# A new order of the work behind entry 288, in an attention and MLP-mixer kernel that replays a written order

## The chip, the core and the metric

The program runs on one core of one Trainium2 chip. The core has a matrix engine (PE, with its weight loads shown apart as PEld), a vector engine (DVE), a scalar engine (ACT), a general engine (POOL) and a synchronisation engine (SP). Each works through its own list of instructions in order, and they wait for one another by semaphores. Inputs and output lie in the chip's HBM; transfers between it and the on-chip memory are DMAs, issued here by POOL, SP and ACT. The metric is the device time of one execution in microseconds, as the median over runs.

## What is computed

There are 8 samples of 576 positions. A block-causal attention with 8 heads of width 64 gives x (576 x 512 per sample); then an MLP mixer follows, first over the positions and then over the channels. Cut to what matters, the reference is:

```python
scores = np.matmul(q, k.transpose(0, 1, 3, 2)) / np.sqrt(64)       # q, k, v: (8, 8, 576, 64)
mask = block_i >= block_j                                          # blocks of 64 positions
attn = np.exp(np.where(mask, scores, -1e9) - max); attn /= sum     # over the last axis
x = np.matmul(attn, v)  # heads side by side: (8, 576, 512)
h = np.maximum(x.transpose(0, 2, 1) @ w_tok1, 0.0) @ w_tok2        # 576 -> 256 -> 576
u = x + h.transpose(0, 2, 1)
out = u + np.maximum(u @ w_ch1, 0.0) @ w_ch2                       # 512 -> 1536 -> 512
```

## The kernel before

**Operations and the table.** The function first makes a list of 1526 numbered operations, each with its possible engines, the operations that it depends on, and a small function that emits its instructions. Then `placed` walks a table of words, `ORDER`, and the kernel emits the operations in the table's order. A word such as `1479D` means: emit operation 1479 now, on DVE (T is PE, A is ACT, P is POOL, S is SP). Letters behind it, as in `1488Tgd`, name the PSUM banks that the operation takes: a to d are the tiles `mm0` to `mm3`, e to h the tiles `late0` to `late3`. Since every engine works in order, the table fixes the order of each engine's list, which engine does a move that two engines could do, and which bank is used. Waits follow from the data: an engine stands still at the first instruction whose input or buffer is not ready. Nothing decides at run time.

**The stages.** Per sample: q and k are loaded by POOL (L417) and transposed by DVE in 288-column pieces (L440). `score_set` multiplies them on PE (L562) in three sets per group of four heads; it uses the array in strips of 32 rows. ACT takes the exponential out of PSUM (L777). POOL or DVE copies and clears masked parts (L588, L599). `head_out` multiplies by v on PE (L616), `ends_out` does the last 64 rows (L669) with half of the array's columns; DVE divides by the sum (L636 and L642, L691 and L697). `token_up` (L814, L818) and `token_mix` (L913, L944) are the mixer's first half; SP transposes its result by DMA (L980). `channel_up`, `channel_up_half` (L1114) and `channel_up_fast` (L1238) are the first channel product, the last two with seven products in place of eight (differences made by DVE, sums folded from PSUM, L1153, L1271). `channel_down_fast` (L1372) is the second channel product, also with seven products; DVE makes its operand sums (L1354) and folds each result into the output tile `o_sb` (L1396), and SP or ACT writes it (L1438; L1424 for the shared tile of the samples' last 64 rows). Later samples' attention is interleaved on PE with earlier samples' mixer.

**The end of the program.** Three jobs of `channel_down_fast` stand there. Operations 1466 to 1483 are the shared tile of last rows; its writes are 1480, 1481, 1482 and 1483, each of 256 KB from 64 partitions. Operations 1488 to 1504 and 1509 to 1525 are the last sample in two halves: products 1490, 1492, 1494, 1496, 1498, 1500 and 1511, 1513, 1515, 1517, 1519, 1521 (six matmuls each), each followed by the fold with the next number, and writes 1502 and 1523 (256 KB each), 1503, 1504, 1524 and 1525 (128 KB each). Fold 1479 completes the output tile of writes 1482 and 1483.

Of the kernel before, what the change touches and what calls it, by code (L numbers as in the profile page):

```python
# [27 lines left out]
class Plan:  # L28
# [74 lines left out]
    140D 82P 161P 53Td 141D 146A 60Td 147Td 137D 129D 130D 166A 151Tc 152T 148T 134D 46Ta 44Ta 202Tabef 206A 204A
    205A 164D 185D 175Tg 153D 154D 155Th 149D 176D 177D 156D 157D 267Tc 268D 150D 203A 265Tg 167Th 208Tcbfe 266A
    187P 168T 81P 88P 87P 84P 83P 171Tg 89P 210A 269Td 209A 270A 90P 172T 211A 86P 85P 212A 343P 188D 273Tb 189D
    169D 170D 186D 277Th 173D 241Tdcaf 245A 174D 271Tg 10P 274D 244A 242A 275Tb 281Tf 278D 279Th 272D 285Tg 280A
    276D 195Tbdae 198A 197A 4D 282D 5D 286D 283Th 284D 310Tf 319Tg 287Th 288A 316Td 295Ta 317T 318D 320T 196A 243A
    322Th 323T 321A 199A 228Tdcbg 324A 200D 289Te 207D 290T 232A 230A 261D 296T 297A 6D 345D 311T 312D 231A 191P
    229A 192P 301Tc 193P 262D 346P 302T 235Taghb 239A 291A 236A 292Td 293T 233D 190P 194P 201P 344D 304Tb 294D 305T
    348D 234D 298Te 299T 347D 352P 216Td 219Ta 220D 237A 303A 217D 218D 213Tc 222Tg 306A 214D 223D 300A 238A 215D  # L110
    240D 225Th 226D 224D 367Tdebf 370A 227D 221D 313Tc 314T 369A 255Th 315D 373Tagbe 246Tc 368A 353D 371A 375A 354D
    307Td 376A 349P 247D 377A 256D 91P 248D 252Tf 308T 309A 257D 350D 351D 374A 258Tb 253D 360Tcegh 362A 361A 259D
    522P 364A 254D 334Td 249Te 519P 250D 251D 338Tf 393Thcae 260D 428Tb 395A 263D 264D 363A 520D 523D 396A 429D 397A
    394A 398D 426Tc 427A 92P 339T 372P 406Theag 409A 408A 93P 358P 432Tc 524D 433D 434Tb 435D 407A 340T 341D
    400Tceah 410A 430Tg 431D 436Tf 437D 335T 442Tg 404A 444Th 445D 403A 357P 521D 355P 402A 365P 359P 366P 401A
    446Tf 356P 378Tc 379D 387Te 388D 381Th 384Ta 405P 382D 389D 390Tb 447A 443A 380D 528P 391D 383D 392D 438Tg 385D
    399P 423Tc 424D 439A 536Thefb 537A 538A 539A 440Tg 540A 386D 336T 417Ta 425D 325Tc 549Tbfeh 94D 95D 441A 551A
    96D 450D 552A 531P 525P 97D 337D 329Tg 330T 454Tef 532P 553A 685P 451D 550A 533P 418D 535P 331T 411Tb 529D 332D
    527D 412D 413D 326T 420Tg 688P 421D 414Td 457A 460T 461A 469Thb 419D 422D 472A 455Ta 526D 691P 456A 415D 416D
    530D 470Tg 471A 541D 542P 327T 475T 476A 458Tg 452D 328D 453D 473Ta 543Tdhce 700P 459A 462T 687D 464T 474A 479T  # L120
    477T 546A 463D 547A 534P 544A 545A 690D 478D 569Tdgec 573A 572A 571A 701P 689D 480D 602Th 570A 603D 604Tc 605A
    576Thgea 578A 580A 548P 566Td 482T 577A 465D 466D 574D 467T 468A 694P 567D 568D 686D 612Td 613D 483D 582Thagc
    579A 585A 606Tf 857P 586A 557Te 610Td 581D 481D 584A 484Tbg 485Tc 611D 615S 583A 558D 487A 560Ta 559D 448Th 449A
    607D 608Td 486A 561D 609D 614S 490T 488Tf 491A 562D 554Th 692D 489A 563Te 564D 709Tabdc 711A 555D 556D 494T 342S
    565D 495D 492T 493D 575P 593Te 594D 590Th 591D 587Tb 588D 592D 710A 713A 712A 714P 497T 595D 498D 715Tdfca 333S
    589D 854P 599Th 596Te 597D 496A 697P 699P 695D 598D 716A 600D 719A 601D 870P 718A 696D 499D 500D 503Tgd 717A
    501D 504A 702Tebca 704A 616D 620Tfh 698P 623A 706A 863P 505T 693D 860P 705A 703A 707D 626T 627A 635Tab 507Tc
    638A 502D 641T 642A 506D 509T 508D 748Tgafe 751A 511T 617D 510D 512D 749A 859D 618D 858D 954P 752A 750A 513T
    735Tcaeg 736A 739A 708D 867P 770Tf 619D 514D 771A 855D 636Tc 737A 637D 856D 738A 740P 639Tg 515T 516D 742Tecaf
    862D 640A 645T 646D 745A 726Td 727D 643T 644D 865D 746A 720Ta 868P 768Tf 648T 723Tg 769D 721D 744A 728D 724D  # L130
    725D 624Tc 778Tf 722D 779D 774Td 729Tg 730D 731D 625A 628T 649A 776Ta 743A 747P 621Te 622A 777D 780Tg 781A 775D
    732Ta 783S 871Tdefb 874A 873A 875A 733D 629D 772Tg 647D 734D 741P 753Tc 773D 630T 650Tfa 653A 872A 762Tg 631D
    651Tb 652A 861D 759Te 754D 633T 755D 763D 764D 656T 657D 760D 761D 654Tb 634A 655A 878Tgchd 880A 879A 881A 864D
    765Tf 766D 660T 767D 756Te 757D 661D 658T 782S 819Tgf 758D 882A 822A 517S 804Thc 964P 807A 663T 659D 785D 786D
    789Tde 664A 792A 825T 632D 790Tb 787D 826A 662D 665D 951P 965P 960P 808Ta 809A 791A 866P 795T 796D 805Tg 810T
    806A 812T 813D 811A 793Tb 794A 814T 815D 917Thdga 799T 788D 876P 800D 797T 798D 918A 666D 919A 920A 921A 869P
    957P 820Th 817T 818A 823Tg 824A 802T 803A 967P 884Tabdc 888A 886A 821D 885A 887A 883P 667D 829T 827T 669Teh 670A
    830D 832T 956D 833A 828D 953D 904Tdabc 907A 877P 901Tg 668D 906A 902D 905A 955D 903D 908A 963P 952D 1051P 671T
    672D 911Tdabf 912A 914A 961D 895Tg 896D 897D 898Tc 899D 892Te 893D 915A 913A 900D 894D 937Td 938A 889Tg 981Tcafb
    985A 916D 909P 910P 890D 931Te 958D 932D 933D 984A 982A 673Td 891D 934Tg 983A 816A 959D 1057P 968Tecfb 970A 935D  # L140
    966P 936D 674D 972A 922Ta 923D 1054P 971A 924D 925Tg 926D 962D 1060P 927D 969A 675T 676D 928Ta 1066P 929D
    1008Tgfbc 1010A 677T 1011A 973P 1012A 1009A 930D 678D 975Tabfe 977A 979A 1053D 683S 679T 978A 1014Tebdg 1052D
    976A 680D 1015A 1017A 1055D 1016A 831D 939Tf 940D 1001Teacd 1018A 1002A 1004A 1062D 980P 974P 992Tb 986Tf 1003A
# [12 lines left out]
    1279D 1166T 1167A 1187Tc 1177D 1188A 1189T 1190A 1184Tf 1185D 1138Tdb 1198Tge 1292Th 1293D 1141A 1191T 1192D
# [1430 lines left out]
```

## Time and profile before

| | |
|---|---|
| median of 3 runs | 284.12 us (284.1 to 284.63) |
| the profiled execution: span from first to last instruction | 282.2 us |
| PE busy | 275.3 us (98%), 3580 matmuls |
| DVE busy | 238.8 us (85%), 523 instructions |
| ACT busy | 177.8 us (63%) |
| POOL busy | 78.8 us (28%) |
| read from HBM and written to it | 35.85 MB and 9.44 MB |

The profiled execution's span is 1.9 us shorter than the median time: what lies around the first and the last instruction is not in the profile. A line of a group names the source line, the engine, the operation, the tiles and shapes, the count, the busy time and the mean of one; behind the bar stands the engine's idle time before it. The chain of waits follows the work that ended last backwards, to what released each piece. A matmul's record is longer than the distance to the next one, since they are pipelined; so PE's speed is read from the starts.

### The profile page before, as it was taken

To read this page: it belongs to the slowest core of one execution; us is meant where nothing else is said; L and a number is where in the kernel's file an instruction comes from. 1 tells how busy PE (TensorE), PEld (TensorE's weight loads), DVE (VectorE), ACT (ScalarE), POOL (GpSimd) and SP (SyncE) were. 2 spreads that over 40 slices of the span, in tenths; PEclk is the share of its full clock that TensorE was granted. 3 is DMA by queue.
4 is the path that set the end of the run, shared out by engine and by line. 5 is a ranking of instruction groups with operands and counts; after the bars stand their busy time and mean duration, and the time that the engine had idled before them with its cause. 6 is when DMAs were issued, how large, how long until landed. Compare 5 with 4: busy or idle time off the path is not lost.

```text
span 282.2 us, 8544 instructions
## 1 busy us (share of the span) xinstructions
PE 275.3 (98%) x3580; PEld 193.2 (68%) x3580; DVE 238.8 (85%) x523; ACT 177.8 (63%) x326; POOL 78.8 (28%) x131
## 2 busy tenths in 40 slices
PE   7899999999999999999999999999999999999994
PEld 2457665475768877888776658744589664788884
DVE  4589598889889989999988879887797898898974
ACT  4788888775899774899997990326840858530000
POOL 8876726371613422092257210000000000000000
PEclk9999999999999999999999999999999999999999
DMA  8999999959958947699399465150127200020555
GB/s 160 167 153 194 191 200 203 162 63 170 95 88 229 150 67 56 151 104 127 46 118 161 31 141 120 42 114 19 37 49 210 80 0 0 3 75 14 212 126 174
DMA packets 64918, 31.75 MB, mean 112 GB/s; under 512 B 53104, under 2 KB 56176, under 8 KB 64880
## 3 DMA queue, kind: packets, MB, share of 16 engines
q0 software_dynamic: 45040, 17.64, 54.0%
q1 hardware_dynamic: 19408, 12.91, 16.7%
q10 hardware_dynamic: 432, 0.66, 0.7%
q8 instruction: 28, 0.46, 0.7%
q14 instruction: 10, 0.08, 0.1%
HBM read 35.85 MB, written 9.44 MB: 160 GB/s over the span
## 4 chain that ended last, share of the span: by engine, by line
PE 82%; DMA 10%; DVE 3%; ACT 2%; POOL 1%; issue 1%; DVEq 0%; POOLq 0%
PE mm L1372 13%; PE late L1372 11%; DMA qk_sb<-in_q_dram 7%; PE late L1114 7%; PE late L1238 6%; PE mm L1114 6%; PE mm L1238 6%; PE mm L562 4%; PE late L616 3%; DMA wc_sb<-in_moe_w_ch_dram 3%; PE late L562 3%; PE late L913 3%; PE mm L814 2%; PE mm L616 2%; PE late L814 2%; PE mm L913 2%
## 5 line engine op out<-in xcount | busy, mean ns | idle before, releaser
L777 ACT ACTIVATE e_sb<-mm 128x512 bf16<-128x512 f32 x94 | 53.5, 612 | 9.8 <-PE mm L562 4.2
L777 ACT ACTIVATE e_sb<-late 128x512 bf16<-128x512 f32 x74 | 43.0, 613 | 5.6 <-PE late L562 2.7
L440 DVE STREAM_TRANSPOSE qk_sb<-qk_sb 128x288 int32<-128x288 int32 (+2 forms) x57 | 38.3, 695 | 6.0 <-ACT qk_sb L393 1.9
L469 POOL DMA_DIRECT2D vals<-in_v_dram x45 | 37.1, 833 | 8.5 <-PE late L616 7.5
L1372 PEld LDWEIGHTS <-sums 128*128 128x128 bf16 x288 | 27.8, 98 | 4.2 <-issue 0.4
L1372 PEld LDWEIGHTS <-gT 128*128 128x128 bf16 x288 | 27.9, 98 | 3.7
L562 PEld LDWEIGHTS <-qk_sb 32*64 32x64 bf16 (+1 forms) x1024 | 16.9, 99 | 16.5 <-issue 9.6
L562 PE MATMUL mm<-qk_sb 32*64 32x320 bf16 (+6 forms) x534 | 27.7, 273 | 0.0
L616 PEld LDWEIGHTS <-e_sb 128*128 128x128 bf16 x640 | 23.9, 97 | 5.4 <-issue 0.9
L393 ACT COPY late<-mm 128x512 f32<-128x512 f32 (+1 forms) x14 | 8.0, 571 | 27.6 <-DVE o_sb L1396 14.5
L562 PE MATMUL late<-qk_sb 32*64 32x320 bf16 (+6 forms) x382 | 25.0, 277 | 0.3 <-DVE x_sb L642 0.3
L1114 PEld LDWEIGHTS <-ws_sb 128*128 128x128 bf16 x192 | 17.9, 98 | 4.2 <-issue 0.9
L599 POOL MEMSET e_sb<- 64x512 bf16 (+1 forms) x23 | 11.4, 511 | 31.7 <-ACT e_sb L777 28.4
L800 ACT ACTIVATE gT<-late 128x512 bf16<-128x512 f32 x20 | 12.2, 611 | 7.4 <-PE late L1114 4.9
L1114 PEld LDWEIGHTS <-wc_sb 128*128 128x128 bf16 x144 | 15.5, 113 | 1.8
L1238 PEld LDWEIGHTS <-ws_sb 128*128 128x128 bf16 x96 | 9.4, 98 | 9.8
L616 PE MATMUL late<-vals,e_sb 128*128 128x65 bf16 x360 | 15.8, 193 | 0.0
L642 DVE TENSOR_TENSOR x_sb<-late,rinv 128x256 bf16<-128x256 f32 x36 | 14.8, 418 | 0.7
L580 ACT ACTIVATE e_sb<-sc 128x1024 bf16<-128x1024 f32 x11 | 10.8, 1026 | 4.5 <-PE sc L562 4.5
L1372 PE MATMUL mm<-wd_sb,sums 128*128 128x256 bf16 x108 | 13.1, 273 | 0.0
L616 PE MATMUL mm<-vals,e_sb 128*128 128x65 bf16 x280 | 12.4, 193 | 0.0
L417 POOL DMA_DIRECT2D qk_sb<-in_k_dram x12 | 6.6, 551 | 20.7 <-ACT e_sb L777 7.1
(203 smaller groups left out, 649.4 us busy)
## 6 DMA issues: line engine op xcount, KB each, us to landing
out_dram<-o_sb SPq DMA_DIRECT2D x14, 512.0 KB, 3.0
vals<-in_v_dram POOLq DMA_DIRECT2D x28, 128.0 KB, 5.9
qk_sb<-in_k_dram POOLq DMA_DIRECT2D x12, 288.0 KB, 5.6
qk_sb<-in_q_dram POOLq DMA_DIRECT2D x12, 288.0 KB, 6.1
wc_sb<-in_moe_w_ch_dram POOLq DMA_DIRECT2D x8, 192.0 KB, 7.8
wc_sb<-in_moe_w_ch_dram POOLq DMA_DIRECT2D x3, 512.0 KB, 8.0
out_dram<-o_sb SPq DMA_DIRECT2D x4, 256.0 KB, 3.2
vals<-in_v_dram POOLq DMA_DIRECT2D x15, 64.0 KB, 5.4
```

The source lines that it names most:

```text
L440: nc.vector.transpose(dst[:, 0:S, :] .rearrange("p s e -> p (s e)") .bitcast(I32) .rearrange("p (a k) -> p k a", k=NB)[:, k0:k1], raw2.bit ...
L469: nc.gpsimd.dma_start(out=t[128 - p : 128, J, hs, 0:64], in_=src)
L562: nc.tensor.matmul(out=home(n)[rows, c : c + w], lhsT=kT[i][r, 64 * j : 64 * j + keys, par], rhs=qT[i][r, 64 * q : 64 * q + w, par], start ...
L599: (nc.vector if o.engine == "DVE" else nc.gpsimd).memset(late_keys, 0.0)
L616: nc.tensor.matmul(out=u[:, I, 0:65], lhsT=e[:, h, c : c + 128], rhs=vt[:, J, head, 0:65], start=(J == 0), stop=(J == I),)
L642: nc.vector.tensor_tensor(out=xt[:, 0:4, 64 * head : 64 * head + 64], in0=u[:, :, 0:64], in1=ri[:, 0:4].to_broadcast([128, 4, 64]), op=MULT,)
L777: nc.scalar.activation(dst, bank_of(x), EXP, scale=scale)
L800: nc.scalar.activation(dst, src, RELU)
L913: nc.tensor.matmul(out=bank_of(bank), lhsT=w2_sb[:, t, 128 * si : 128 * si + 128], rhs=at[:, t, :], start=(t == 0), stop=(t == NDT - 1),)
L1114: nc.tensor.matmul(out=bank_of(bank)[:, 256 * o_ : 256 * o_ + 256], lhsT=x(o_, m), rhs=y[:, :, m, :], start=opens, stop=m == 1, skip_group ...
L1238: nc.tensor.matmul(out=bank_of(bank), lhsT=x(m), rhs=y[:, :, m, :], start=first and m == 0, stop=m == 1, skip_group_check=not first,)
L1372: nc.tensor.matmul(out=bank_of(bank)[:, 256 * i : 256 * i + 256], lhsT=x[:, kk, 128 * i : 128 * i + 128], rhs=y[:, kk], start=first and i ...
```

## The change

The table's first 288 words stay as they are; behind them the same operations stand in another order. The number of operations and of matmuls is the same, and each operation emits as many instructions as before. 63 moves out of PSUM change between DVE and ACT (32 to ACT, 31 to DVE), and 12 copies and clears between DVE and POOL (6 each way). Of the table, its end is shown.

```diff
--- before
+++ after
 ORDER = """
     9D 8D 14S 7D 0A 15A 11S 41Ta 19P 69Tb 17P 1D 52Tb ...
     ...
-    1468T 1469D 1412S 1474T 1475D 1480S 1476T 1477D 1486D 1515T 1511T 1478T 1481S 1488Tgd 1507D 1508D 1513Tf 1479D
-    1483S 1489A 1516D 1519T 1514D 1520D 1517T 1482A 1512D 1492Tc 1524S 1518D 1523A 1494T 1493D 1487D 1495D 1490T
-    1491D 1496T 1497D 1502S 1498T 1499D 1503S 1521T 1500T 1522D 1501D 1525S 1504A
+    1513Te 1506D 1485D 1469D 1494T 1475D 1412S 1495D 1476T 1510D 1515T 1492Ta 1481S 1486D 1477D 1478T 1487D
+    1498T 1516D 1480S 1507D 1508D 1514D 1493D 1499D 1519T 1520D 1524S 1511T 1479D 1483S 1512D 1490T 1491D 1503S
+    1500T 1482A 1501D 1517T 1518D 1523A 1521T 1522D 1525S 1496T 1497D 1502S 1504A
 """
```

Source lines of the changed kernel stand 3 further down, because the table is three lines longer.

**The end, DVE.** DVE's last rows before; the first one is fold 1479, the row with `um_sb`, and two more rows follow what is shown.

```order
L1396 TENSOR_TENSOR o_sb0<-mm2,um_sb_65 128x2x256
L1396 TENSOR_TENSOR o_sb1<-late3,e_sb0 128x256
L1396 TENSOR_TENSOR o_sb2<-late1,e_sb0 128x256
L1396 TENSOR_TENSOR o_sb2<-late3,o_sb2 128x256
L1396 TENSOR_TENSOR o_sb1<-late0,e_sb0 128x256
L1396 TENSOR_TENSOR o_sb1<-late1,o_sb1 128x256
L1396 TENSOR_TENSOR o_sb2<-mm2,e_sb0 128x256
L1354 TENSOR_TENSOR vals_62<-vals_62 128x6x128
L1396 TENSOR_TENSOR o_sb1<-mm3,e_sb0 128x256
L1396 TENSOR_TENSOR o_sb1<-late2,e_sb0 128x256
L1396 TENSOR_TENSOR o_sb1<-mm2,o_sb1 128x256
L1396 TENSOR_TENSOR o_sb2<-mm3,o_sb2 128x256
```

DVE's last rows in the change, to the end of its list.

```order
L1357 TENSOR_TENSOR vals_62<-vals_62 128x6x128
L1399 TENSOR_TENSOR o_sb2<-late0,e_sb0 128x256
L1399 TENSOR_TENSOR o_sb2<-mm0,e_sb0 128x256
L1399 TENSOR_TENSOR o_sb2<-mm3,o_sb2 128x256
L1399 TENSOR_TENSOR o_sb2<-late3,o_sb2 128x256
L1399 TENSOR_TENSOR o_sb0<-mm2,um_sb_65 128x2x256
L1399 TENSOR_TENSOR o_sb1<-late2,e_sb0 128x256
L1399 TENSOR_TENSOR o_sb1<-late1,e_sb0 128x256
L1399 TENSOR_TENSOR o_sb2<-mm3,e_sb0 128x256
L1399 TENSOR_TENSOR o_sb1<-late0,o_sb1 128x256
L1399 TENSOR_TENSOR o_sb2<-late3,e_sb0 128x256
L1399 TENSOR_TENSOR o_sb1<-mm0,o_sb1 128x256
```

Fold 1479 had 13 instructions behind it and now has 6; the row ahead of it is now fold 1520.

**The end, SP.** SP's last rows before: the output writes. Rows of 64x2x512 are the shared tile's.

```order
L1438 DMA out_0_dram<-o_sb2 128x2x512
L1438 DMA out_0_dram<-o_sb1 128x2x512
L1424 DMA out_0_dram<-o_sb2 64x2x512 x2
L1424 DMA out_0_dram<-o_sb0 64x2x512
L1438 DMA out_0_dram<-o_sb2 128x256
L1438 DMA out_0_dram<-o_sb1 128x512
L1438 DMA out_0_dram<-o_sb2 128x256 x2
```

And in the change.

```order
L1441 DMA out_0_dram<-o_sb2 128x2x512
L1441 DMA out_0_dram<-o_sb1 128x2x512
L1427 DMA out_0_dram<-o_sb2 64x2x512 x2
L1441 DMA out_0_dram<-o_sb2 128x256
L1427 DMA out_0_dram<-o_sb0 64x2x512
L1441 DMA out_0_dram<-o_sb2 128x256 x2
L1441 DMA out_0_dram<-o_sb1 128x512
```

The write from `o_sb0` now stands behind a write of the last sample, and SP's last write is the one of 128x512 (write 1502). ACT's list ends as before with writes 1482, 1523 and 1504.

**The middle, POOL.** These are POOL's rows around 135 to 150 us, where it loads the last sample's q and k and the sample before's v. Before:

```order
L469 DMA vals_62<-in_v_dram 128x8x64
L417 DMA qk_sb_61<-in_k_dram 128x1152
L588 COPY vals_62<-e_sb1 128x256
L599 MEMSET e_sb1 64x4x2x64
L417 DMA qk_sb_61<-in_k_dram 128x1152
L469 DMA vals_62<-in_v_dram 128x8x64
L417 DMA qk_sb_61<-in_q_dram 128x1152 x2
L469 DMA vals_62<-in_v_dram 128x8x64
L588 COPY vals_62<-e_sb0 128x256
L599 MEMSET e_sb0 64x4x2x64 x2
```

In the change:

```order
L591 COPY vals_62<-e_sb1 128x256
L420 DMA qk_sb_61<-in_q_dram 128x1152
L420 DMA qk_sb_61<-in_k_dram 128x1152
L420 DMA qk_sb_61<-in_q_dram 128x1152
L472 DMA vals_62<-in_v_dram 128x8x64 x2
L591 COPY vals_62<-e_sb0 128x256
L602 MEMSET e_sb0 64x4x2x64
L472 DMA vals_62<-in_v_dram 128x8x64
L591 COPY vals_62<-e_sb1 128x256
L602 MEMSET e_sb1 64x4x2x64
L420 DMA qk_sb_61<-in_k_dram 128x1152
```

The two q loads (operations 1054 and 1060) stood behind both k loads and a v load, and now the first of them is the first of the four. A v load (operation 966) now stands behind the copy and the clear of `e_sb0`, which wait for exponentials.

**The middle, DVE.** DVE's rows ahead of the first score set of the seventh sample's first group, operation 968, in the change. The last row frees the bank that this score set needs.

```order
L443 STREAM_TRANSPOSE qk_sb_61<-qk_sb_61 128x9x32 x3
L805 TENSOR_SCALAR gT1<-mm2 128x2x256
L443 STREAM_TRANSPOSE qk_sb_61<-qk_sb_61 128x9x32
L1357 TENSOR_TENSOR sums1<-sums0,gT0 128x1536
L1399 TENSOR_TENSOR o_sb1<-late2,u_sb2 128x2x256
L443 STREAM_TRANSPOSE qk_sb_61<-qk_sb_61 128x9x32
L639 RECIPROCAL rinv3<-mm1 128x4
L645 TENSOR_TENSOR x_sb2<-mm1,rinv3 128x4x64
L443 STREAM_TRANSPOSE qk_sb_61<-qk_sb_61 128x9x32
L639 RECIPROCAL rinv2<-late1 128x4
L645 TENSOR_TENSOR x_sb2<-late1,rinv2 128x4x64
```

Before, the same rows of DVE around that `rinv2`:

```order
L440 STREAM_TRANSPOSE qk_sb_61<-qk_sb_61 128x9x32
L691 RECIPROCAL rinv8<-late2 128x2
L440 STREAM_TRANSPOSE qk_sb_61<-qk_sb_61 128x9x32
L697 TENSOR_TENSOR x_sb2<-late2,rinv8 128x128
L440 STREAM_TRANSPOSE qk_sb_61<-qk_sb_61 128x9x32
L1396 TENSOR_TENSOR o_sb1<-late0,u_sb2 128x2x256
L440 STREAM_TRANSPOSE qk_sb_61<-qk_sb_61 128x9x32
L636 RECIPROCAL rinv2<-late2 128x4
L642 TENSOR_TENSOR x_sb2<-late2,rinv2 128x4x64
```

In the change a ReLU of the channel product (L805) and an operand sum (L1357) stand between the transposes ahead of this row.

More of the change, by code (lines that the diff above doesn't have):

```diff
@@ L103 @@
[L103 to L107, printed above, removed]
@@ L173 @@
[L173 to L174 removed]
+    9D 8D 14S 7D 0A 15A 11S 41Ta 19P 69Tb 17P 1D 52Tb 21P 31P 25P 51Tb 65Tb 23P 29P 12A 27P 3D 2D 16D 20D 18D
+    22D 13D 26D 24D 105Ts 106A 98Ttbc 61Td 57Td 49Td 99A 100D 30D 63Td 118A 122Ts 70Td 123A 78Td 62Td 54Td 102Tt
+    103A 45Td 28D 104D 35P 34P 50Td 33P 158Ts 159A 142Tt 143A 32P 74Td 181P 178P 101D 55Td 115Td 68Tb 125Ts
@@ new lines @@
+    543Tdebc 546A 411Th 412D 479T 477T 413D 480D 544A 478D 545A 417Tb 418D 455Td 547A 548P 456A 482T 576Tcaeh
+    700P 458Td 483D 419D 687D 560Tg 561D 563Tb 577A 580A 686D 564D 562D 554Tc 602Th 579A 459A 481A 462T 697P
+    603A 555D 556D 578A 464T 565D 463D 699P 465D 569Tcegb 570A 572A 557Td 571A 604Ta 605A 689D 558D 559D 467T
+    466D 484Tce 468A 573A 690D 487D 582Tdgha 581P 606Tf 608Tb 692D 607D 854P 490T 701P 585A 609D 612Th 613D
+    485Tf 610Tb 584A 611D 488Tg 695D 574P 575P 696D 586A 566Th 567D 491A 583A 486A 489A 709Tabcf 710A 494T 492T
@@ new lines @@
+    897D 801D 890D 915A 891D 914A 968Tbcdf 972A 893D 673Te 676D 971A 969A 894D 981Tadfg 985A 667D 674D 909P
+    939Tb 983A 677T 958D 959D 910D 970A 916D 984A 982A 678D 940A 1054P 975Tcdfg 977A 1051P 1052D 979A 934Ta
+    928Tb 931Te 925Td 935D 978A 1060P 936D 932D 933D 937Ta 976A 929D 831A 964P 963P 930D 922Tg 1001Tbcef 668D
+    938A 926D 927D 973P 923D 679T 1053D 924D 980D 1004A 974P 1003A 680D 1002A 1005A 1055D 1008Taced 966P 1010A
+    1009A 986Tb 1012A 1006P 989Tg 1056D 987D 988D 681T 682D 1014Tdcfa 683S 1011A 992Tb 990D 1018A 995Te 1034Th
@@ new lines @@
+    1080P 1114Taegb 1117A 1118A 1040Tc 845D 1116A 842Tf 1041D 950S 848T 1115A 1108Tabec 942D 949S 843D 1110A
+    1074P 1089Tg 849D 1086Td 1087D 1088D 1111A 846T 1095Tb 1048S 1112A 1109A 1092Td 1113D 1093D 850T 1106P
+    1270Ta 1096D 1097D 1107P 1094D 1090D 1091D 1271A 847D 1131Tg 1098Tb 1049S 1119Tf 851D 1132D 1099D 1100D
+    1133D 1122Tc 1168Tad 1128Te 1123D 1124D 1171A 1125Tb 1268Tg 1126D 1129D 1174T 1120D 1269A 1121D 1134D
+    1153Thc 1169Tf 1156A 1175A 1170A 1130D 1276Te 1127D 1274Tb 1135D 1136D 1282Tg 1275D 1283D 1159T 1172Ta 1173A
```

128 lines of the change are left out of this document (59 added, 69 removed).

## The prediction

> **What bounds the kernel now.** I read the page's head, then the span by stages, then the chain of waits, and last the end of the timeline.
>
> ```profile
> span 282.2 us, 8544 instructions
> PE 275.3 (98%) x3580; PEld 193.2 (68%) x3580; DVE 238.8 (85%) x523; ACT 177.8 (63%) x326; POOL 78.8 (28%) x131
> ```
>
> PE is busy for 98% of the span, so I cut the span at the first moved matmul (42.19 us) and at PE's last one (278.65):
>
> ```profile
> 0.00:42.19 42.19, 39.11 (x608) 23.12 (x609) 30.25 (x88) 32.10 (x52) 28.88 (x53) 1.00 1.30 178
> 42.19:278.65 236.46, 236.14 (x2977) 170.12 (x2972) 208.12 (x435) 145.72 (x274) 49.95 (x79) 1.00 0.63 101
> 278.65:282.20 3.55, 0.00 (x0) 0.00 (x0) 0.42 (x1) 0.00 (x0) 0.00 (x0) 0.98 0.34 116
> ```
>
> The columns are the length, the busy time of PE, PEld, DVE, ACT and POOL, the granted clock, the DMA share and GB/s. In the moved part PE has 236.46 - 236.14 = 0.32 us with nothing running, at a clock of 1.00. A new order can therefore gain little there: it can lose by new waits, and it can change the 3.55 us behind PE's last matmul. So I look for three things: waits that go, waits that come, and the end.
>
> The distances on PE, from the chain of waits:
>
> ```profile
> 85.88 0.60 PE late L616 x20
> 86.48 0.57 PE mm L562 x16
> ...
> 212.43 2.62 PE late L1372 x24
> 215.05 0.44 PE mm L1114 x4
> ```
>
> A `head_out` (ten matmuls) takes 0.30 us, a score set 0.57, a group of six matmuls of the second channel product 0.655 (twelve: 1.31), a product of L1114 0.44.
>
> **The wait that goes.** The longest chain through another engine in the moved part is this one:
>
> ```profile
> 143.94 7.26 DMA qk_sb<-in_q_dram
> ...
> 152.40 0.70 DVE qk_sb L440
> ...
> 153.16 0.77 DVE x_sb L642 x2
> 153.93 0.04 issue
> 153.97 0.30 PE late L562
> ```
>
> A q load of the last sample lands at 151.20; the transposes that it feeds hold up DVE's in-order list, the two multiplies behind them free a PSUM bank late, and a score set starts at 153.97. PE's rows there, and PE's largest waits that lie in the moved part:
>
> ```profile
> 151.75 1.47 PE L1372 MATMUL late<-wd_sb,gT 128*128 128x256 bf16 x12
> 153.15 0.32 PE L669 MATMUL mm<-vals,e_sb 128*64 128x65 bf16 x8
> ```
>
> ```profile
> PE late L562 <- DVE x_sb L642: 0.3, 1, 0.3
> PE late L669 <- ACT e_sb L777: 0.2, 1, 0.2
> ```
>
> Twenty matmuls of `ends_out` from 153.15 are through by 153.56, so the stall is 0.4 us. In the change both q loads stand ahead of the k and v loads behind which they were queued, by POOL's rows some 6 us earlier (134.6 and 137.3 where they were 141 and 143.9). That is more than DVE was late by: this term is -0.4. The bounds are -0.3 (the waits view) and -0.4 (the starts).
>
> **The waits that come.** Each is set by whether DVE, ACT or POOL gets to a bank or a tile before PE's denser list asks for it. The largest is score set 968, whose bank `late1` comes free only with multiply 897. DVE's prices:
>
> ```profile
> L440 DVE STREAM_TRANSPOSE qk_sb<-qk_sb 128x288 int32<-128x288 int32 x55 | 37.7, 704 | 5.3 <-ACT qk_sb L393 1.9 <-DMA qk_sb<-in_k_dram 1.3 <-DMA qk_sb<-in_q_dram 1.2
> ...
> L1153 DVE TENSOR_TENSOR gT<-late,half 128x512 bf16<-128x512 f32 x12 | 8.1, 684 | 0.2 <-ACT e_sb L777 0.2
> ...
> L1354 DVE TENSOR_TENSOR sums<-gT 128x1536 bf16<-128x1536 bf16 x6 | 5.7, 953 | 0.1
> ...
> L642 DVE TENSOR_TENSOR x_sb<-late,rinv 128x256 bf16<-128x256 f32 x36 | 14.8, 418 | 0.7
> ...
> L636 DVE RECIPROCAL rinv<-late 128x4 f32<-128x4 f32 x36 | 5.8, 170 | 1.7 <-PE late L616 1.6
> ...
> L1168 DVE TENSOR_SCALAR gT<-gT 128x1024 bf16<-128x1024 bf16 x10 | 4.2, 419 | 0.0
> ```
>
> Between product 814 and set 968 DVE now has 26 instructions without a free stretch: 9 wide ones of 0.684, 3 ReLUs of 0.419, 2 sums of 0.95, 6 transposes of 0.704, two pairs of reciprocal and multiply (0.17 + 0.418) and the smaller pair of the end rows (0.44): 15.2 us. Neighbours overlap by 0.08 (two folds of 0.42 start 0.34 apart, the rows at 273.39 and 273.73 below), 25 times: 13.2. Inside the run it waits some 0.45 for products and within the pairs, and it starts 0.2 behind product 814: 13.85. PE meanwhile has ten products (4.4), three jobs of twelve matmuls (3.93), four score sets (2.3), four `head_out` (1.2), a `token_mix` and an `ends_out` (1.1), and five changes of the array's mode (0.09 each, below): 13.4. So 968 is 0.45 late, and what stands behind it on PE (product 673, set 981) with it; DVE's next rows don't need 968, so nothing is paid twice. The same count at other places gives smaller ones: set 904 waits about 0.2 for three exponentials behind set 884 (with 1.75 us of PE between), and products 799 and 610 and sets 497, 1008 and 986 would be 0.1 to 0.25 late each. Their sum is 0.8, but a stall taken earlier gives the next engine its time back, and the list before has waits of this size too, of which PE's rows show only the 0.2 of L669. I take +0.2 for them together, +0.65 with 968. Bounds: 0 for all (the wide ones overlap more) and +1.25 (968 and all of the others).
>
> **Mode changes.** The job at 151.75 takes 1.40 us to the half-column `ends_out` behind it, where 1.31 is its work: entering that mode costs 0.09. By the order, entries from full-array work into it grow from 7 to 9 (entries from score sets, which cost nothing visible, fall from 6 to 4); entries into the 32-row strips stay at 35. +0.2; bounds 0 and +0.2.
>
> **The 63 and 12 moves between engines.** DVE gains 31 and loses 32 evacuations of like size, POOL and DVE exchange six; DVE's total stays at about 208 us under 236 of PE, which is what hides it. Where the cover is gone locally is the item above. 0.
>
> **The end.** The last rows of the timeline, issues included:
>
> ```profile
> 271.43 0.69 DVE L1396 TENSOR_TENSOR o_sb<-mm,um_sb 128x512 f32<-128x512 f32 x1 [0.53 <-PE mm L1372]
> ...
> 272.14 0.59 SPq L1424 DMA_DIRECT2D out_dram<-o_sb  x1
> ...
> 273.39 0.42 DVE L1396 TENSOR_TENSOR o_sb<-late,o_sb 128x256 f32<-128x256 f32 x1 [0.23 <-PE late L1372]
> 273.73 0.41 DVE L1396 TENSOR_TENSOR o_sb<-late,e_sb 128x256 f32<-128x256 f32 x1
> ...
> 278.67 0.42 DVE L1396 TENSOR_TENSOR o_sb<-mm,e_sb 128x256 f32<-128x256 f32 x1 [0.25 <-PE mm L1372]
> ```
>
> Fold 1479 (271.43) lets the writes 1483 and 1482 go at 272.14, 6.5 us before PE's end. In the change it stands behind fold 1520, and PE has six groups behind product 1519: 6 x 0.655 = 3.93. Fold 1520 ends 3.5 us before PE's end, fold 1479 (0.69, less the overlap) 2.9 before: the two writes go at -2.8, 3.7 us later, counted from PE's end. By the same count the rest goes at -3.4 (1524), -2.2 (1503), -0.8 (1523), -0.6 (1504), -0.2 (1525) and +0.5 (1502). The last write is now 1502 with 256 KB, where it was 1504 with 128 KB. What the DMA engines do there (share is the next to last column):
>
> ```profile
> 272.00:273.00 1.00, 1.00 (x12) 0.90 (x10) 0.71 (x3) 0.36 (x1) 0.00 (x0) 1.00 0.00 0
> ...
> 273.00:277.50 4.50, 4.50 (x44) 4.01 (x42) 3.49 (x10) 0.00 (x0) 0.00 (x0) 1.00 0.77 204
> 277.50:281.00 3.50, 1.13 (x11) 0.75 (x8) 1.11 (x3) 0.00 (x0) 0.00 (x0) 1.00 0.55 192
> ...
> 280.20:280.40 0.20, 0.00 (x0) 0.00 (x0) 0.00 (x0) 0.00 (x0) 0.00 (x0) 1.00 0.88 297
> ```
>
> and single writes there, with size and us to landing (the first is 1502, the second the last one, 1504, the third 1524):
>
> ```profile
> out_dram<-o_sb SPq DMA_DIRECT2D x1, 256.0 KB, 2.1
> ...
> out_dram<-o_sb ACTq DMA_DIRECT2D x1, 128.0 KB, 1.7
> ...
> out_dram<-o_sb SPq DMA_DIRECT2D x1, 128.0 KB, 4.4
> ```
>
> The eight last writes (1536 KB) take 0.77 x 4.5 + 0.55 x 3.5 = 5.4 us of all DMA engines. First packets come about 1.1 us after an issue (none until 273.0 behind the issue at 272.14). Before, nearly all is through when the last write goes; that one is issued at 279.13, moves its last data at 280.4 and has landed at 280.85, 2.2 us after PE's end. In the change write 1524 is through early; the other seven (1408 KB) start at -2.83 + 1.1 = -1.7 and take 4.1 us (at 192 / 0.55 = 349 GB/s) to 5.0 (5.4 less 0.4 for write 1524). They end at +2.4 to +3.3, and land 0.43 later, at +2.8 to +3.7 instead of +2.2: +0.6 to +1.5. I take the middle, +1.0. The bounds are +0.4, if the last write lands by itself (2.1 instead of 1.7), and +1.6, if all data were as slow as the mean of 273 to 277.5 (204 / 0.77 = 265 GB/s: 5.4 us). The rule that speaks against the low bound is in the Trainium skill, "DMA: Bandwidth & Descriptors", section "Queues, rings and completion order": each DMA engine takes turns between its queues, and the write that reports a transfer lands only after that engine's earlier writes. By it the last write can't report ahead of the seven, which gives +1.0; without it, +0.4. The trace agrees so far: write 1524 of 128 KB took 4.4 us behind others, where 1504 took 1.7.
>
> **Sum.** -0.4 + 0.65 + 0.2 + 1.0 = +1.45 against the profiled 282.2: a span of 283.7. The median of the runs, 284.12, lies 1.9 above the span, for what is outside the profile; I carry that over: 284.12 + 1.45 = 285.6.
>
> **The rivals.**
> A, the writes are hidden after all: the DMA engines interleave so well that only the larger last write counts (+0.4), the new waits come to +0.4 and cancel the one that goes, and the mode entries cost 0.1. +0.5: 284.6. For it speaks the 2.1 us of write 1502 behind others; against it the 4.4 of 1524.
> B, faster: the order removes all stalls of PE's rows in the moved part, 0.4 at 153 and the 0.2 and 0.1 of smaller ones, brings none, and the end is level because the eight writes run at full rate while PE is still working. -0.7: 283.4. It decides if DVE's overlap at 968 is above 0.1 an instruction. Against it stands that fold 1479 is late by order, whatever the rate.
> C, slower by a load: value load 966 stands in POOL's list behind a copy and a clear that wait for an exponential of set 968.
>
> ```profile
> L599 POOL MEMSET e_sb<- 64x512 bf16 x22 | 11.1, 521 | 31.6 <-ACT e_sb L777 28.4 <-DVE vals L588 1.5 <-PE late L562 1.1
> ...
> L588 POOL COPY vals<-e_sb 128x256 bf16<-128x256 bf16 x7 | 3.1, 446 | 8.8 <-ACT e_sb L777 6.3 <-issue 2.4
> ```
>
> ```profile
> vals<-in_v_dram POOLq DMA_DIRECT2D x28, 128.0 KB, 5.9
> ```
>
> ```profile
> vals<-in_v_dram POOLq DMA_DIRECT2D x5, 128.0 KB, 7.9
> ```
>
> The load goes 1.0 us behind that exponential; set 975 starts 0.5 behind it, and from there to `head_out` 986, the first reader, PE has two score sets, six smaller jobs and a product, 5.9 us. So there is room for 5.4. The median of all such loads is 5.9 (+0.5, inside the bounds of the waits), but the five from 42 to 60 us had 7.9 as their median: then PE stands for 2.5 us, and 284.12 + 1.45 + 2.5 = 288.1. Against it: q, k and v loads no longer bunch here as they did at 141 to 145.
>
> **How the numbers follow.** Chances: forecast 0.66, A 0.17, B 0.07, C 0.10. A measurement of this kernel tells about 0.2%, 0.57 us, from no change: 283.55 to 284.69. The forecast is slower but for 0.02, A is no change but for 0.01, C slower, B faster: faster 0.07, same 0.18, slower 0.75. The range: at the low end the low bound of the end (+0.4) with the waits about even gives 284.3; at the high end 1.6 + 0.2 - 0.4 + 1.25 = 2.65, 286.8, and some of the case between forecast and C, 287.0. C's full price and B stay outside, 17 in 100.
>
> **What would show it.** In the changed profile: writes 1482 and 1483 issued about 2.8 us before PE's last matmul, and the span's end some 1.0 us further from PE's end than the 3.55 now; the last landing at +2.8 or later. PE's end at 279.1 (278.65 + 0.45), with no chain through a q load near 150 us, and a wait of 0.3 to 0.5 for `x_sb` (897) at set 968. If PE ends later than 280.3, a wait I have not seen, or C, was the cause; if the end behind PE is under 3.9, A holds; if PE ends before 278.2, B does.

## The result and the profile after

The changed kernel takes 287.25 us (median of 4 executions, 287.18 to 287.46), the kernel before 284.22 beside it: a ratio of 1.0113, with a 95% interval of 1.0094 to 1.0132. It is slower by 3.0 us. The forecast was slower by 1.45, and the measured time lies just outside the range (284.3 to 287.0).

The head of its page:

```profile
span 285.3 us, 8518 instructions
PE 273.9 (96%) x3557; PEld 192.8 (68%) x3580; DVE 240.8 (84%) x522; ACT 179.7 (63%) x327; POOL 79.3 (28%) x131
```

(23 matmul records are missing from this trace; the weight loads show all 3580.) The span cut in the same way as before, at the first moved matmul and at the end of the last one; the columns are length, busy time of PE, PEld, DVE, ACT and POOL, granted clock, DMA share and GB/s:

```profile
0.00:42.24 42.24, 38.23 (x606) 23.07 (x610) 30.49 (x88) 32.07 (x52) 29.59 (x54) 1.00 1.30 178
42.24:279.80 237.56, 235.68 (x2958) 169.76 (x2972) 209.84 (x434) 147.59 (x275) 49.71 (x78) 1.00 0.63 97
279.80:285.30 5.50, 0.00 (x1) 0.00 (x0) 0.42 (x1) 0.00 (x0) 0.00 (x0) 0.92 0.62 208
```

The unmoved stretch is as long as before, the moved part is 237.56 where it was 236.46 (+1.1), and the end behind PE 5.50 where it was 3.55 (+1.95). These two make the 3.1 us between the spans. All kernels below are read by the same two stretches, since the unmoved stretch alone took 41.8 to 43.3 us from one profile to the next.

**Where the moved part lost.** PE's largest new wait, and the chain of waits around it:

```profile
PE mm L1117 <- DVE mm L398: 0.5, 1, 0.5
```

```profile
127.68 0.45 PE late L1117 x4
...
128.75 0.70 DVE mm L398
129.46 0.04 issue
129.50 0.60 PE mm L1117 x4
```

Product 827 could have followed at 128.83 and starts at 129.50; product 802 behind it is 0.15 late as well. The DVE copy that it needs (operation 824, on ACT in the kernel before) starts at 128.75, because two ReLUs ahead of it in DVE's list took twice their time. DVE's and POOL's rows there; the third fence gives count and the shortest, median and longest duration of the two:

```profile
126.34 1.51 DVE L1171 TENSOR_SCALAR gT<-gT 128x1024 bf16<-128x1024 bf16 x2
```

```profile
126.27 0.52 POOL L602 MEMSET e_sb<- 64x512 bf16 x1
126.73 1.58 POOL L472 DMA_DIRECT2D vals<-in_v_dram  x2
```

```profile
L1171 DVE TENSOR_SCALAR gT<-gT x2: 735/792/849, 126.3 to 127.0; 128x1024 bf16<-128x1024 bf16 x2
```

The others of this form took about 420 ns, in both kernels: so 0.75 us of DVE time is lost here, beside a clear and two value loads issued by POOL. Three smaller waits follow. At set 968 three of the four row strips start and the fourth, whose bank multiply 897 frees, starts 0.31 later:

```profile
139.75 0.33 PE L565 MATMUL mm<-qk_sb 32*64 32x320 bf16 x3
140.06 0.30 PE L565 MATMUL late<-qk_sb 32*64 32x320 bf16 x1
```

Head 986 waits 0.22 for value load 966, which lands 6.21 us after its issue:

```profile
145.36 6.21 DMA vals<-in_v_dram
```

And set 1114 loses 0.27, since its banks come free only with the exponentials of set 1101, which PE has left 1.6 us earlier. The stall of 0.4 at the q load is gone, and some 0.3 of smaller ones near 90, 150 and 163 us: 0.82 + 0.29 + 0.22 + 0.27 - 0.7 = 0.9, and the rest of the 1.1 are the entries into PE's array modes (some 0.095 us for one into half columns, nine of them where there were seven).

**Where the end lost.** The last rows:

```profile
276.25 0.68 DVE L1399 TENSOR_TENSOR o_sb<-mm,um_sb 128x512 f32<-128x512 f32 x1
276.36 0.35 SPq L1441 DMA_DIRECT2D out_dram<-o_sb  x1
...
276.96 0.60 SPq L1427 DMA_DIRECT2D out_dram<-o_sb  x1
276.96 0.73 ACTq L1427 DMA_DIRECT2D out_dram<-o_sb  x1
...
279.84 0.42 DVE L1399 TENSOR_TENSOR o_sb<-mm,o_sb 128x256 f32<-128x256 f32 x1 [0.23 <-PE mm L1375]
```

Fold 1479 runs at 276.25, and writes 1483 and 1482 go at 276.96, 2.84 us before PE's end at 279.80. What moves behind them, and how long writes 1483 and 1482 and the last, 1502, take to land:

```profile
278.00:283.25 5.25, 1.80 (x17) 1.37 (x14) 1.57 (x4) 0.00 (x0) 0.00 (x0) 1.00 0.93 271
```

```profile
out_dram<-o_sb SPq DMA_DIRECT2D x1, 256.0 KB, 3.4
out_dram<-o_sb ACTq DMA_DIRECT2D x1, 256.0 KB, 4.8
```

```profile
out_dram<-o_sb SPq DMA_DIRECT2D x1, 256.0 KB, 3.7
```

From 278.0 to 283.25 the DMA engines are 93% busy at 271 GB/s: 1.42 MB, all of the seven late writes but the last packets. Write 1502, issued 0.49 behind PE's end, lands 4.2 behind it; the last write before, 1504, landed at 2.2.

### The profile page after: what moved, and what is told of

The parts are those of the page before. It is cut to its first block, busy times and chain, and to the rows that moved or that the text cites. A ratio compares the mean times of both kernels' runs of the same rounds, so it can differ in the third digit from the quotient of the medians.

```text
span 285.3 us, 8518 instructions
## 1 busy us (share of the span) xinstructions
PE 273.9 (96%) x3557; PEld 192.8 (68%) x3580; DVE 240.8 (84%) x522; ACT 179.7 (63%) x327; POOL 79.3 (28%) x131
## 4 chain that ended last, share of the span: by engine, by line
PE 80%; DMA 2%; issue 1%; DVE 0%; ACT 0%; DVEq 0%
PE late L1375 15%; PE mm L1375 11%; PE late L1117 8%; PE mm L1241 7%; PE late L1241 6%; PE mm L565 6%; PE mm L1117 5%; PE mm L619 3%; PE mm L817 3%; PE mm L916 3%; PE late L619 2%; DMA vals<-in_v_dram 2%; PE late L1466 2%; PE mm L1466 2%; PE mm L672 1%; PE late L565 1%
## 5 line engine op out<-in xcount | busy, mean ns | idle before, releaser
L780 ACT ACTIVATE e_sb<-mm 128x512 bf16<-128x512 f32 x90 | 52.0, 610 | 10.7 <-PE late L565 4.9
L780 ACT ACTIVATE e_sb<-late 128x512 bf16<-128x512 f32 x78 | 44.4, 609 | 10.6 <-PE late L565 7.7
L565 PE MATMUL late<-qk_sb 32*64 32x320 bf16 (+6 forms) x412 | 27.0, 276 | 0.0
L803 ACT ACTIVATE gT<-mm 128x512 bf16<-128x512 f32 x18 | 10.9, 617 | 9.8 <-PE mm L1117 8.6
L1117 PEld LDWEIGHTS <-wc_sb 128*128 128x128 bf16 x144 | 15.4, 113 | 1.6 <-issue 0.4
L619 PE MATMUL mm<-vals,e_sb 128*128 128x65 bf16 x380 | 16.3, 193 | 0.2
L645 DVE TENSOR_TENSOR x_sb<-mm,rinv 128x256 bf16<-128x256 f32 x38 | 15.7, 419 | 0.9
L591 POOL COPY vals<-e_sb 128x256 bf16<-128x256 bf16 x10 | 4.2, 418 | 39.4 <-ACT e_sb L780 25.9
L1375 PE MATMUL late<-wd_sb,sums 128*128 128x256 bf16 x120 | 14.8, 273 | 0.0
L931 DVE TENSOR_TENSOR u_sb<-mm,x_sb 128x512 bf16<-128x512 f32 x17 | 11.3, 685 | 3.5 <-PE mm L916 3.3
L1241 PEld LDWEIGHTS <-wc_sb 128*128 128x128 bf16 x72 | 7.9, 113 | 5.9 <-issue 0.2
```

The source lines that it names most:

```text
L565: nc.tensor.matmul(out=home(n)[rows, c : c + w], lhsT=kT[i][r, 64 * j : 64 * j + keys, par], rhs=qT[i][r, 64 * q : 64 * q + w, par], start ...
L619: nc.tensor.matmul(out=u[:, I, 0:65], lhsT=e[:, h, c : c + 128], rhs=vt[:, J, head, 0:65], start=(J == 0), stop=(J == I),)
L645: nc.vector.tensor_tensor(out=xt[:, 0:4, 64 * head : 64 * head + 64], in0=u[:, :, 0:64], in1=ri[:, 0:4].to_broadcast([128, 4, 64]), op=MULT,)
L780: nc.scalar.activation(dst, bank_of(x), EXP, scale=scale)
L803: nc.scalar.activation(dst, src, RELU)
L931: nc.vector.tensor_tensor(out=ut[:, si, :], in0=bank_of(bank), in1=xt[:, si, :], op=ADD)
```

## The experiments

The kernels of the first four were run beside one another, and so were the next four. Each ratio is against the kernel before, run beside them (284.23 us, 284.10, and 284.03 for the last). A diff shows the words of the order table.

**The clear, away from the ReLUs.** On the changed kernel:

```diff
-876P 866P 827T
+876P 877P 866P 827T
...
-962D 877P 965P
+962D 965P
```

> The changed kernel with one word moved: POOL's clear 877 (the 64x512 MEMSET that ran at 126.27 us) stands right behind copy 876, so that it runs some 2.9 us earlier and no longer beside DVE's two ReLU rows (TENSOR_SCALAR, 128x1024 bf16) which took 735 and 849 ns there where the others take 417. Theory 1 (the clear and DVE's ReLU hold each other up): both rows go back to about 420 ns, DVE's copy ahead of product 827 is 0.7 us earlier, PE's wait of 0.8 us there (0.67 + 0.15) goes, and the kernel is 0.6 to 0.8 us faster than the change, about 286.5. Theory 2 (it is the value loads that POOL issues at 126.7 and 127.6, which stay where they are): one or both rows stay at 735 to 849 ns and the time stays at 287.2. Theory 3 (PE's wait goes but comes back at set 968, which waits for the same DVE list): rows at 420, time within 0.2 of 287.2.

The two ReLUs and POOL's rows beside them (this execution's unmoved stretch was 1.04 us longer, so all rows stand that much later):

```profile
L1174 DVE TENSOR_SCALAR gT<-gT x2: 407/570/733, 127.4 to 128.1; 128x1024 bf16<-128x1024 bf16 x2
```

```profile
126.96 1.98 POOL L475 DMA_DIRECT2D vals<-in_v_dram  x2
```

```profile
43.27:280.20 236.93, 235.57 (x2958) 169.62 (x2972) 209.53 (x434) 147.60 (x275) 50.17 (x78) 1.00 0.62 98
```

One of them is back at 407, the other still takes 733, without a clear near it, but starting 0.44 us into the first value load (of 0.92 us). So theories 1 and 2 are each half right: both kinds of POOL's work hold the ReLU up. The wait at product 827 fell from 0.67 to 0.22, and the moved part from 237.56 to 236.93; 0.22 of that is the wait at head 986, which this execution doesn't show. The time, 286.96 (ratio 1.0096, 1.0069 to 1.0123), agrees but is too coarse for it.

**Fold 1479 earlier.** On the changed kernel:

```diff
-1508D 1514D 1493D 1499D 1519T 1520D 1524S 1511T 1479D 1483S 1512D 1490T 1491D 1503S 1500T 1482A 1501D
+1508D 1514D 1479D 1483S 1482A 1493D 1499D 1519T 1520D 1524S 1511T 1512D 1490T 1491D 1503S 1500T 1501D
```

> The changed kernel with fold 1479 moved up in DVE's list to behind fold 1514, and the writes 1483 and 1482 with it (1483 ahead of 1524 on SP). The two writes can go about 1.55 us earlier, 4.4 us before PE's last matmul where it is 2.83. Theory 1 (the end is set by the transfer of the last writes, 1408 KB at some 266 KB per us from the first packet of write 1483 on): the last landing moves from 4.2 us behind PE's end to 2.7 and the kernel is 1.3 to 1.6 us faster than the change, about 285.8. Theory 2 (the size and the issue of the last write alone set the end): no change, 287.2.

The stretch behind PE, and the last write:

```profile
279.16:283.20 4.04, 0.00 (x1) 0.00 (x0) 0.42 (x1) 0.00 (x0) 0.00 (x0) 0.83 0.54 195
```

```profile
out_dram<-o_sb SPq DMA_DIRECT2D x1, 256.0 KB, 2.2
```

The end is 1.46 shorter, as theory 1 had it, and the last write now lands in 2.2 us, as one alone did before. Time 286.06, ratio 1.0062 (1.0042 to 1.0082).

**The smaller write last.** On the changed kernel, the fold left late:

```diff
-1503S 1500T 1482A 1501D 1517T 1518D 1523A 1521T 1522D 1525S 1496T 1497D 1502S 1504A
+1503S 1496T 1482A 1497D 1502S 1517T 1518D 1523A 1521T 1522D 1525S 1500T 1501D 1504A
```

> The changed kernel with the last products in another order, so that write 1502 (256 KB) goes about 2 us before PE's end and the last write is 1504 (128 KB), as in the kernel before; fold 1479 and writes 1483 and 1482 stay late. Theory 1 (the transfer of all late writes sets the end): they carry the same bytes from the same start, so the end behind PE stays at 5.3 to 5.5 us; time within 0.3 of 287.2. Theory 2 (the last write's own size): 0.4 or more faster, 286.8 or below.

```profile
280.11:285.70 5.59, 0.00 (x1) 0.00 (x0) 0.42 (x1) 0.00 (x0) 0.00 (x0) 0.91 0.61 205
```

```profile
out_dram<-o_sb ACTq DMA_DIRECT2D x1, 128.0 KB, 3.8
```

Half the bytes in the last write gain nothing: it lands 3.8 us after its issue, behind the others, where it took 1.7. Time 287.6, ratio 1.0114 (1.009 to 1.0138); end and time lie 0.1 above what theory 1 allowed, and theory 2 falls.

**Fold 1479 later, in the kernel before.**

```diff
-1513Tf 1479D 1483S 1489A 1516D 1519T 1514D 1520D 1517T 1482A 1512D 1492Tc 1524S 1518D 1523A 1494T 1493D 1487D
+1513Tf 1489A 1516D 1519T 1514D 1520D 1517T 1512D 1492Ta 1524S 1518D 1523A 1494T 1493D 1479D 1483S 1482A 1487D
```

> The kernel before with fold 1479 alone moved back in DVE's list to behind fold 1493, the writes 1483 and 1482 with it (and product 1492 in bank a, since 1479 frees bank c later). The two writes go about 2.85 us before PE's end where it was 6.5. Writes 1524 and 1523 go as before. Theory 1 (transfer sets the end): 1152 KB from 1.75 us before PE's end at 266 KB per us end 2.6 behind it and land at 3.0, where it was 2.2: 0.8 us slower than the kernel before (0.5 to 1.2), about 285.0. Theory 2 (the last write's own size): no change, 284.2.

```profile
43.04:279.19 236.15, 235.04 (x2958) 169.99 (x2972) 208.11 (x435) 145.76 (x274) 49.80 (x79) 1.00 0.62 99
279.19:283.90 4.71, 0.00 (x0) 0.00 (x0) 0.42 (x1) 0.00 (x0) 0.00 (x0) 0.96 0.55 174
```

The one moved fold costs 1.14 us at the end (4.71 instead of 3.55 and 3.59 in the two profiles of the kernel before), more than the 0.8 expected, inside the 0.5 to 1.2. Time 285.24, ratio 1.0032 (1.0014 to 1.005). Its moved part shows something else: 236.15, since the wait at set 1068 isn't there, though nothing ahead of it was changed; the q load landed in 6.6 us, not in 7.26.

**The kernel before, again.** No edit.

> The kernel before, once more, for a second profile. The question is what repeats. If the wait of 0.4 us at 153 us (score set 1068 behind the transposes of the late q load) is set by the order alone, it stands there again and the part from the first moved matmul to PE's last one takes 236.4 us. If it hangs on how fast that one load lands (7.26 us in the first profile), it can be absent, as in the run with the late fold, and the part takes some 236.1. The end behind PE is 3.5 to 3.6 either way.

```profile
42.75:279.11 236.36, 234.91 (x2958) 170.04 (x2972) 208.19 (x435) 145.76 (x274) 50.09 (x79) 1.00 0.63 100
279.11:282.70 3.59, 0.00 (x0) 0.00 (x0) 0.42 (x1) 0.00 (x0) 0.00 (x0) 0.82 0.34 116
```

```profile
144.49 7.19 DMA qk_sb<-in_q_dram
...
153.63 0.77 DVE x_sb L642 x2
154.40 0.04 issue
154.44 0.30 PE late L562
```

The q load takes 7.19 us, and the stall is there again, 0.4 as before: PE's twenty matmuls of `ends_out` start at 153.60 and are through by 154.0, and the score set starts at 154.44. So this wait goes with the load's landing: 0.4, 0.4 and none with 7.26, 7.19 and 6.6 us in three profiles of this middle. The end repeats to 0.04.

**The q loads earlier, in the kernel before.**

```diff
-909P 910P 890D 931Te 958D 932D
+909P 910P 890D 931Te 962D 1060P 1054P 932D
...
-816A 959D 1057P 968Tecfb
+816A 958D 968Tecfb
...
-923D 1054P 971A 924D 925Tg 926D 962D 1060P 927D
+923D 971A 924D 925Tg 926D 959D 1057P 927D
```

> The kernel before with the three DVE transposes 962, 958, 959 in this order in the places where 958, 959, 962 stood, and POOL's q loads 1060 and 1054 right behind the first of them, so that they are issued at about 140 us where it was 143.9 and 142.8 (the k load 1057 and the v load 966 come behind them). DVE's and PE's lists are otherwise the same. Theory of the prediction (the late q load costs 0.4 us): the part from the first moved matmul to PE's end takes 236.0 where it was 236.4, and the time is 0.2 to 0.4 us below the kernel before. Rival (DVE's rows behind the transposes were about to be late anyway, by something else): 236.4 and no change.

```profile
139.63 1.07 POOL L423 DMA_DIRECT2D qk_sb<-in_q_dram  x2 [2.12 <-DVE rinv L642]
```

```profile
41.99:277.93 235.94, 234.83 (x2957) 169.86 (x2972) 208.35 (x435) 145.76 (x274) 50.09 (x79) 1.00 0.63 101
277.93:281.50 3.57, 0.00 (x0) 0.00 (x0) 0.42 (x1) 0.00 (x0) 0.00 (x0) 1.00 0.35 118
```

The q loads go about 4 (1060) and 2.5 us (1054) earlier, and the moved part is the shortest of all: 235.94, 0.4 to 0.5 below the two profiles of the kernel before. The time is 283.74 against 284.1, ratio 0.9989 (0.9968 to 1.0009): the sign expected, but not told from no change.

**No POOL work on the ReLUs at all.** On the changed kernel, beside the edit of the clear:

```diff
-952D 954P 955D
+952D 869P 954P 955D
...
-906A 869P 913A
+906A 913A
```

> The changed kernel with POOL's clear 877 right behind copy 876 and value load 869 ahead of loads 954 and 957: DVE's two ReLU rows near 126.3 us then have neither a clear nor the second half of a value load beside them; only the issue of a k load and the first quarter microsecond of a value load. Theory (POOL's clears, and its value loads from about 0.23 us after their start on, exclude DVE's bf16 ReLU, whoever comes first goes first): both rows take 410 to 430 ns where it was 735 and 849, PE's wait of 0.67 at product 827 goes below 0.1 and the moved part takes 236.7 to 236.9 us where it was 237.57. Rival (the value load holds DVE up for its whole 0.9 us, or any issue on POOL does): at least one of them stays above 500 ns.

```profile
L1174 DVE TENSOR_SCALAR gT<-gT x2: 419/424/430, 126.5 to 126.9; 128x1024 bf16<-128x1024 bf16 x2
```

```profile
42.42:279.56 237.14, 235.46 (x2958) 169.74 (x2972) 209.22 (x434) 147.61 (x275) 49.90 (x78) 1.00 0.62 97
```

```profile
144.81 6.52 DMA vals<-in_v_dram
```

Both ReLUs are at their usual time beside the issue of a k load, and the wait at product 827 is gone (0.08 stays at product 802). The moved part fell only to 237.14, not to 236.8: PE now reaches head 986 0.7 us earlier while its value load doesn't land earlier, and waits 0.53 there instead of 0.22. Time 286.19, ratio 1.007 (1.0043 to 1.0096).

**The middle of the change with the end of the kernel before.** The first 1453 entries of the changed table, then the rest in the old order.

```diff
 (entries 0 to 1452 of the changed table)
-1509Tgh ... 1502S 1504A   (the changed order)
+1509Tgh 1510D 1464D 1465D ... 1501D 1525S 1504A   (the order before)
```

> The first 1453 entries of the changed table, and then what is left in the order of the table before (with banks g, h for product 1509 and e for 1513): the middle of the change with the end of the kernel before. If the two parts of the loss are independent, the end behind PE goes back from 5.5 to 3.5 to 3.7 us, the moved part stays at 237.4 to 237.7, and the time is 1.9 us below the change: 285.3. If the end of the kernel before needs its own middle (DVE or ACT late there), the end stays above 4.2 or PE stops in the last 15 us.

```profile
42.27:282.63 240.36, 236.07 (x2958) 169.70 (x2972) 210.22 (x434) 147.61 (x275) 49.84 (x78) 1.00 0.62 99
282.63:286.20 3.57, 0.00 (x1) 0.00 (x0) 0.43 (x1) 0.00 (x0) 0.00 (x0) 1.00 0.35 117
```

```profile
PE mm L1378 <- DVE o_sb L1402: 1.8, 1, 1.8
```

The end is back at 3.57, but PE stops near 268 for some 1.9 us and again, for 0.6 and 0.3, at 276 and 277: the folds and operand sums of the end don't fit behind this middle. Time 288.2, ratio 1.0131 (1.01 to 1.0163). As a test of the middle alone it failed; it shows that the end of the kernel before isn't to be had by pasting it.

**All three repairs together.** On the changed kernel: the edits of the clear and value load, of fold 1479, and value load 966 ahead:

```diff
-964P 963P 930D
+964P 963P 966P 930D
...
-1008Taced 966P 1010A
+1008Taced 1010A
```

> The changed kernel with three edits together: POOL's clear 877 and value load 869 moved as in the run for the ReLU rows, fold 1479 with writes 1483 and 1482 moved up as in the run for the fold, and value load 966 right behind the two value loads ahead of it on POOL, in front of copy 973, so that it is issued at about 142.2 us where it was 145.4. Theory (the loss is the sum of these waits): PE's wait at product 827 is gone (below 0.1), that at head 986 is gone (0.24 in the change, 0.54 once the ReLU rows were free), set 968 and set 1114 keep their 0.29 and 0.27; the part from the first moved matmul to PE's end takes 236.5 to 236.7 us where it was 237.57, the end behind PE 4.0 to 4.1 where it was 5.5. Against the change that is 0.95 + 1.45 = 2.4 us, time about 284.9, some 0.6 above the kernel before: what is left is 0.47 for the larger last write and the two score sets. Rival (each wait taken away hands its time to the next): the moved part stays above 237.0.

```profile
42.60:279.20 236.60, 235.30 (x2958) 169.64 (x2972) 209.17 (x434) 147.58 (x275) 49.90 (x78) 1.00 0.63 98
279.20:283.20 4.00, 0.00 (x0) 0.00 (x0) 0.42 (x1) 0.00 (x0) 0.00 (x0) 1.00 0.55 197
```

Both stretches came out as expected, and the waits at product 827 and head 986 are gone while those at sets 968 and 1114 stay (0.29 and 0.27). Time 285.07, ratio 1.0032 (1.0018 to 1.0047): 1.0 us above the kernel before, where 0.6 was expected and the change had 3.0, so moving six words of the table wins back some 2.0. No repair of the change got below the kernel before.

## Why the prediction was wrong

The direction and the two places, the waits and the end, were right; both terms were too small, and together they were half of what was measured.

**The end, +1.0 forecast, +1.95 measured.** The issue times came out to within 0.05 us (writes 1483 and 1482 at -2.84, 1502 at +0.49), but for write 1504 (-0.42 where I had -0.6), and the packets start at -1.6 where I had -1.7. What failed is the step from bytes to time: I took the middle between 4.1 us (at 349 GB/s, the rate of the last stretch before) and 5.0, and the seven writes take 5.45, from 278.20 to 283.65, at 265 GB/s. The engines are 91% busy in that time, 4.96 us. So the 5.0, the engine time of these writes before, was the right figure and not the middle, and the 0.5 us in which engines stand idle I had put at nothing.

The bound of +1.6 for all data at 265 GB/s was worked out wrongly: 5.4 us from -1.7 end at +3.7 and land at +4.1, which is +1.9, and the range's high end would have been 287.3. The right row was there, the 204 GB/s at a share of 0.77 from 273.0 on. In it write 1483 is slow in both kernels: 209 and 188 GB/s in the half microseconds from 273.5 and 274.0 before, 197 and 156 from 278.5 and 279.0 in the change, with the engines 93% busy or more, where 350 to 385 are reached later. Why that write is slow no run shows. Rival A (only the larger last write, +0.4) fell with the runs on the fold and on the smaller last write; it is the right price once the fold is early: 4.00 and 4.04 against 3.55 to 3.59.

The rule of the Trainium skill that I cited ("DMA: Bandwidth & Descriptors", section "Queues, rings and completion order") has the last write report behind the earlier ones, which agrees: the last one issued landed last in every profile. Between the two queues landings don't follow the issues, though: write 1525 of SP, issued at -0.17, landed at +3.3, and 1504 of ACT, issued at -0.42, at +3.75. That the engines take turns between queues isn't what the trace shows at first: ACT's write 1482, issued with SP's 1483 at 276.96, had no packet before 279.5; why is open. The queues' rows for 278.0 to 279.4 and for 279.6 to 280.0 (packets, MB, share; q1 is SP's queue, q10 ACT's) have SP's packets alone, and then mostly ACT's:

```profile
q1 hardware_dynamic: 112, 0.23, 84.0%
```

```profile
q10 hardware_dynamic: 44, 0.09, 68.4%
```

**The new waits, +0.65 forecast, some +1.6 measured.** Set 968 was the right place with the right cause, 0.29 instead of 0.45. The +0.2 for all others is the term that failed. Of the six other places named, five wait no more than 0.1, and head 986 waits 0.22, for its value load. Product 827, not named, costs 0.82 with product 802 behind it: there I had priced DVE's ReLUs at 0.419 each from their own row, without looking at what POOL does at that moment. The runs on the clear and on the value load show that it is POOL's work beside them. The Trainium skill bears on it, and I had not weighed it: "SBUF — State Buffer", section "Who interferes with whom", says that VectorE in its two-port modes and GpSimd exclude each other from a shared pair of ports, whoever comes first. The durations of ReLU and clear agree (735 ns instead of 420, and 812 instead of 519 the other way round, below); that this ReLU runs in such a mode no run here shows. Set 1114 (0.27) is of the kind of set 904, exponentials that free a bank late, and was missed in the count.

**The wait that goes, -0.4 forecast.** It went, in all seven profiles with the changed middle; the run with the q loads earlier shows the gain alone, 0.4 to 0.5 in the moved part. But in the kernel before it goes with one load's landing, and one profile in three of its middle doesn't have it. The issue times were misread: the q loads went at 142.8 and 143.9 (141.4 is a k load), and in the change at 137.0 and 139.8, later than I had it but early enough, landing by 145.1.

**Rival C, the late value load.** The mechanism is there, at a tenth to a fifth of its price: load 966 lands in 6.2 and 6.5 us in the two profiles shown, not in 7.9, and head 986 waits 0.22, and 0.53 when PE is earlier. In the run with the smaller write last it waits 0.22 too (6.2 us), and in three other profiles with this load unmoved (5.0 to 6.0 us) it doesn't wait.

**Mode entries, +0.2.** The entries into half columns rose from seven to nine at 0.09; within what the rows can tell this term holds.

**Moves between engines, 0.** DVE is busy 209.84 where it was 208.12 us in the moved part, and 0.75 of that is the two ReLUs. That the moves cost nothing is not shown, and one of them stands at the largest new wait: the DVE copy that product 827 waits for is operation 824, which ACT made in the kernel before (824A there, 824D in the change). The wait goes with the copy still on DVE, once POOL's work is off the ReLUs ahead of it; whether it would also go with the copy back on ACT no run shows.

## What to carry to other kernels

Where PE is 98% busy, as here, a new order is paid for at the few places where another engine's list is as dense as PE's. There a duration from a mean row isn't enough: what POOL does beside DVE's ReLU in the same microsecond belongs in the sum. At the end of a kernel, count the bytes that are still to be written when the last wide write can go, at the rate of the very stretch that these writes had before, and not only the size of the last one: one fold that stands a few rows too late in a list cost 1.46 us here, nearly as much as all new waits in 237 us of matmuls (1.6).

## What the runs showed that was not expected

- DVE's bf16 ReLU from on-chip memory and POOL's clear exclude each other, and the first goes first. With the clear 0.06 to 0.07 us ahead the ReLU takes 735 to 745 ns instead of 420 (four profiles). One that starts 0.25 or 0.35 us into a clear takes 552 or 457 (the kernel before with the late fold, and with the early q loads), and one 0.40 into it the usual 409: so the clear holds it for some 0.38 us of its 0.52. With the ReLU 0.06 ahead, near 109.5 us, the clear takes 812 instead of 519:

```profile
109.50 0.81 POOL L602 MEMSET e_sb<- 64x512 bf16 x1 [2.12 <-ACT e_sb L780]
```

- A value load of 128 KB issued by POOL does the same, but not over its whole 0.9 us. A ReLU that starts up to 0.21 us into it runs at its usual time (the load then takes longer, up to 1.10); one that starts 0.26 into it took 849 to 852, and one 0.44 into it 733. One that starts 0.78 into it is free again. So the span in which the load holds DVE up lies between about 0.25 and 0.75 us; what POOL does in it no run shows.
- The stretch ahead of the first moved entry, the same instructions in every kernel, took 41.8 to 43.3 us. A change of 0.4 us in this kernel is seen in the stretches of a profile, and hardly in a dozen executions.
